# Strip 1's first product by sets, three of them at two levels, and four tiles of attention normalised on ScalarE

## The chip, the cores and the metric

The kernel runs on one core of a Trainium2 chip. A core has a matrix engine (TensorE, PE in the profile, with its weight loads as PEld), a vector engine (VectorE, DVE), an activation engine (ScalarE, ACT), GpSimd (POOL) and SyncE (SP), which here issues nearly all DMAs. Each engine works off its own instructions in order and waits on semaphores for the others. The metric is the device time of one launch in microseconds, lower is better.

## The reference

Everything is fp32. An attention block without softmax feeds a two-layer block with squared ReLU:

```python
kv  = einsum('bhsd,bhse->bhde', k, v)      # B=8, H=8, S=576, D=64
o   = einsum('bhsd,bhde->bhse', q, kv)
o   = o / sqrt(mean(o * o, axis=-1) + 1e-6) * g_norm
x   = o.transpose(0, 2, 1, 3).reshape(4608, 512)
g   = maximum(x @ w_in, 0) ** 2            # w_in  512 x 2048
out = g @ w_out                            # w_out 2048 x 512
```

## The kernel before

The 4608 tokens are cut into 36 tiles of 128, and four tiles make a strip of 512; there are nine strips, 0 to 8. The loop runs strip by strip: the first product of a strip (x by w_in, then relu and square), then its second product (by w_out). While a strip's products run, the attention for the next strip's tiles is worked in between them.

**Products with fewer multiplications.** Both products use a scheme that replaces eight block products by seven, at the price of sums of the inputs and of the results. The seven are numbered and done in the order 1, 2, 6, 5, 7, 3, 4; 1, 6 and 5 leave a partial sum that is copied out of PSUM to a `snap` buffer by ScalarE, and the later ones are added to it. The scheme can be used on two levels: each of the seven is then itself done by seven smaller ones. Strip 0's first product is plain. Strip 1's first product is done at one level by `up(s, g, p)`: four column groups g of w_in, in each the seven products p, each eight matmuls 128x128 by 128x256 in the trace (L839). ScalarE copies (L849), VectorE adds (L902) and squares (L903), ScalarE does relu and square for one quarter (L907, L908). From strip 2 on, the first product is done at two levels by `up_slot`: 55 slots, the outer products as seven sets in the order 1, 6, 7, 5, 2, 3, 4, in each set seven small products of eight matmuls 128x128 by 128x128 (`up_small`, L1283), one in every other slot, neighbouring sets overlapping. In those strips VectorE and GpSimd add (L1295), ScalarE copies (L1300) and does all relu and square (L1233, L1234). The second product is done at two levels from strip 1 on by `down_deep` (matmuls at L1066), which draws small products of its own into slots 49, 51 and 53 of the strip's first product.

**Sums of the weights.** For the two-level first product, GpSimd makes sums of w_in (`deep_sums_in`, seven calls in strip 1, tiles w_i, three instructions each), which SyncE stores to DRAM (`w_in_deep`, L1194 and L1196). Strips from 2 on load them again with `stream()`, the same function that loads the blocks of w_out and their sums; all of these tiles are called w_blk or w_i and share a pool of six buffers. Sums and differences of x (`leaf_x`, tiles x_l and x_t, `deep_differences_in` for w_in) are made by GpSimd and VectorE ahead of their use.

**Attention.** Its pieces stand in a list `slices`, and `attend(n)` works the list off up to number n. For batch 2, whose queries are tiles 9 to 12, and for tile 8, left over from batches 0 and 1, the pieces are: `query_means` for tile 8; `key_value` (K in the list) for the first and second pair of heads; four `transposed_query` (T), each a VectorE transpose of a q tile (L384); `roots_normalized`; `features` for tile 8 (four TensorE transposes, L636, and a ScalarE copy, L637, straight into the strip's x); `key_value` for the other heads; and then for tiles 9 and 10, and again for 11 and 12: `query` (64 matmuls 64x64 into x_ps, L468, then squares on ScalarE, L477), `mean_roots`, `normalized` (reciprocal roots and two VectorE multiplications, L563), `squares_x` (a VectorE transpose by 32x32 blocks, L643), and `send_x` (a store to DRAM, L652, which also puts `fetch_x`, four loads into the strip's x, on a list with a due time). From batch 3 on `normalized` is replaced by `inverse` and `scaled_heads`: eight ScalarE instructions of 128x64 per tile (L570).

**What sets the order.** The program's order on each engine is written by hand. In strip 1 each step of the first product moves a clock on, and after it the strip works off its share of the list:

```python
attend(begun + (goal - begun) * min(i + 1, 25) // 25)
```

Loads of k and v come from a list `keys_due`, one per step where due; loads of q from `drips`, spaced by the same clock. A q tile is loaded by four DMAs (L123) into one of three buffers; `load_q_rest` (L176) loads the left-over queries by eight small ones. All go through SyncE's one queue, in program order, in which also stand the stores of `deep_sums_in` and of `store_deep_sums` (L969, L975), the stores of results (L952) and the loads of weights. Eight semaphores are used in turn for its DMAs, so that an instruction also waits for the DMA eight before it.

Of the kernel before, what the change touches and what calls it, by code (L numbers as in the profile page):

```python
# [20 lines left out]
def kernel(  # L21
# [34 lines left out]
    nc = tc.nc  # L56
# [593 lines left out]
    def send_x(n):  # L650
        d = sent[n] = dram.tile([P, 4, NP, SQ], FP32, name="x_d", tag="x_d", bufs=2 * NT)
        nc.sync.dma_start(out=d, in_=squared.pop(n))  # L652
        tiles_due.append((clock[0] + {9: 30, 10: 36, 11: 24}.get(n, 6), fetch_x, (n,)))
# [53 lines left out]
    slices += [(T, (2, 2)), (T, (2, 3)), (features, (last[0],)), (K, (2, 2, 3))]  # L707
    pair_ends = []
    for b in range(2, B):
        pairs = query_pairs(b)  # L710
        for i, pair in enumerate(pairs):
            left = len(pairs) - i
            more = b + 1 < B
            at = left + (b == 2)
            keys = (b + 1, *{2: (0, 1), 1: (2, 3)}[at]) if more and at < 3 else ()
            if i == 0 and b > 2:
                slices += [(T, (b, p)) for p in (2, 3)]
            if i == 0 and b == 3:
                slices.append((K, (3, 2, 3)))
            if more and b > 2 and left == 1 + b % 2:  # L720
                slices.append((T, (b + 1, 0)))
            slices.append((query, (pair, *keys)))
            if b == 2:
                slices += [(T, (3, 1))] * (left == 1) + [(mean_roots, (pair,)), (normalized, (pair,))]
                slices += [(T, (3, 0))] * (left == 2) + [(squares_x, (n,)) for n in pair]
                for n in pair:
                    slices.append((send_x, (n,)))
                    if n % NT == NT - 1:
                        ready[n // NT] = len(slices)
                pair_ends.append(len(slices))  # L730
# [12 lines left out]
            if more and left == 1:  # L743
                slices.append((T, (b + 1, 1)))
# [144 lines left out]
    def up(s, g, p):  # L889
        open_bank(p)  # L890
        rhs = {
            1: halves(s, 0, 0), 2: halves(s, 1, 0), 3: halves(s, 1, 1),
            4: xc[s][3], 5: xc[s][0], 6: xc[s][1], 7: xc[s][2],
        }[p]
        for i in range(2):
            product(p, i, lambda kc: w_in[:, kc, g, A_IN[p], ts(i, P)], lambda kc: rhs[:, :, kc, :], KH)
        dest = quarters(s, g)

        def relu_squared(q):
            def f(b, a):  # L900
                o = dest[q]
                nc.vector.tensor_tensor(out=o, in0=b, in1=a, op=ALU.add)  # L902
                nc.vector.scalar_tensor_tensor(out=o, in0=o, scalar=0.0, in1=o, op0=ALU.max, op1=ALU.mult)  # L903
            return f

        def last(b):
            nc.scalar.activation(dest[21], b, AF.Relu)  # L907
            nc.scalar.activation(dest[21], dest[21], AF.Square)  # L908

        combine(p, relu_squared(11), relu_squared(12), last, relu_squared(22))  # L910
# [191 lines left out]
    def down_deep(s, k, i):  # L1102
        p = DEEP_ORDER[k]
        if k == i == 0:
            stream()
# [21 lines left out]
        if k == 0 and s >= DEEP_UP:  # L1127
# [52 lines left out]

    def deep_sums_in(b):
# [59 lines left out]
    def up_slot(s, slot):  # L1241

        for n, p in enumerate(UP_SETS):
            i, odd = divmod(slot - 7 * n, 2)
            if not odd and 0 <= i < 7:
# [6 lines left out]
        if s == DEEP_UP and at == 0 and n < 7:  # L1252
# [80 lines left out]
    for s in range(N_STRIP):  # L1333
# [11 lines left out]
        else:  # L1345
            steps = [(1, up, (s, g, p)) for g in range(NG) for p in ORDER]
# [12 lines left out]
        for i, (w, fn, a) in enumerate(steps):  # L1359
# [33 lines left out]
            if s:  # L1393
                clock[0] += 3.2 if i >= n_up else 2.2 if s == DEEP else 1.2
# [5 lines left out]
                elif not due(keys_due) and not (soon and due(tiles_due)):  # L1400
                    least = 2.1 if s == DEEP else 4.5 if i < n_up else 3.3
                    quiet = n_up * 2 // 3 < i < n_up + 3 or s == DEEP and i > n_up + 9
# [4 lines left out]
                if s == DEEP:  # L1407
                    attend(begun + (goal - begun) * min(i + 1, 25) // 25)
# [6 lines left out]
                if s == DEEP and i == n_up - 3:  # L1415
                    leaf_sums(s, 4)
                if s == 1 and i in range(2, 23, 3):
                    deep_sums_in((1, 6, 5, 4, 0, 2, 3)[i // 3])
                if s == 1 and i in (17, 20, 21, 23):
# [60 lines left out]
```

## Time and profile before

| what | value |
|---|---|
| time, median of three runs | 887.08 us (886.7 to 888.0) |
| the profiled execution: time, span | 886.17 us, 884.4 us |
| TensorE busy | 876.4 us (99%), 8296 matmuls |
| VectorE busy | 721.9 us (82%) |
| ScalarE busy | 351.8 us (40%) |
| GpSimd busy | 307.6 us (35%) |
| DMA | 235.73 MB, mean 267 GB/s |
| strip 1's first product | from 138.6 us |
| strip 2's first product, whole | from 236.8 us, its first slots drawn into strip 1's second product |

Busy times are shares of the span of one execution. The list of waits names, for an engine and a line, what ended its idle time there, with the total, the number and the longest. The chain of waits follows the work that ended last. A timeline gives, for one engine, start, duration and instruction, and in brackets the idle time before it with what ended it; for TensorE a run of matmuls is one row, whose duration reaches to the modelled end of its last, so that the distance between the starts of two rows is the rate.

### The profile page before, as it was taken

Reading aid. Unit: us, or ns where it says so; the run is one execution under the profiler, and the core shown is the slowest. Engines: PE = TensorE matmul, PEld = TensorE weight load, DVE = VectorE, ACT = ScalarE, POOL = GpSimd, SP = SyncE. Lnnn points to the kernel's source line nnn. Section 1 sums busy time; section 2 is a strip of 40 time slices with the busy share of each in tenths; the row PEclk is TensorE's granted clock in tenths of the full one; section 3 lists DMA queues with packets and bytes.
Section 4 is the critical chain, followed back from the end, with each engine's and each line's share of the span. In section 5 each row is a group of like instructions: output and inputs, shape, how many; then the busy total and the mean of one; then the engine's idle time right before and its main releaser. Section 6 shows DMA issues by size and latency. Waiting matters only on the chain.

```text
span 884.4 us, 20899 instructions
## 1 busy us (share of the span) xinstructions
PE 876.4 (99%) x8296; PEld 822.1 (93%) x8296; DVE 721.9 (82%) x1239; ACT 351.8 (40%) x805; POOL 307.6 (35%) x316
## 2 busy tenths in 40 slices
PE   8999999999999999999999999999999999999998
PEld 7445888889999999999999999999999999999998
DVE  4999998879778985798778966897888778866887
ACT  4898242320048203740365034902491147102710
POOL 0000005610549133631474045604570447044700
PEclk9999999999999999999999999999999999999999
DMA  9998997999969996989677978897668765884482
GB/s 306 321 314 252 299 376 222 289 346 353 301 186 278 327 330 214 227 323 314 208 216 293 314 237 244 286 319 244 207 218 303 255 212 184 294 292 164 178 314 105
DMA packets 170257, 235.73 MB, mean 267 GB/s; under 512 B 79536, under 2 KB 134576, under 8 KB 161840
## 3 DMA queue, kind: packets, MB, share of 16 engines
q1 hardware_dynamic: 169856, 234.33, 81.0%
q8 instruction: 65, 1.06, 0.5%
q14 instruction: 32, 0.26, 0.1%
q10 hardware_dynamic: 304, 0.07, 0.0%
HBM read 197.66 MB, written 36.70 MB: 265 GB/s over the span
## 4 chain that ended last, share of the span: by engine, by line
PE 95%; DVE 2%; ACT 2%; issue 0%; POOL 0%; DVEq 0%; POOLq 0%
PE ps_B L1066 22%; PE ps_A L1283 19%; PE ps_A L1066 17%; PE ps_B L1283 9%; PE ps_A L839 6%; PE ps_C L1283 5%; PE ps_B L839 3%; PE kv_ps L432 2%; PE ps_A L880 2%; PE x_ps L468 2%; PE ps_C L839 2%; PE ps_C L880 2%; PE ps_B L880 1%; PE ps_A L617 1%; ACT gt L1234 0%
## 5 line engine op out<-in xcount | busy, mean ns | idle before, releaser
L1066 PE MATMUL ps_B<-w_blk,g_s 128*128 128x128 f32 x1008 | 123.9, 275 | 0.0
L1066 PEld LDWEIGHTS ps_B<-w_blk,g_s 128*128 128x128 f32 x1008 | 118.1, 192 | 0.1
L1283 PE MATMUL ps_A<-x_l,w_in 128*128 128x128 f32 x784 | 103.8, 275 | 0.3 <-ACT snap L1300 0.3
L289 POOL TENSOR_TENSOR x_l<-xT 128x256 f32<-128x256 f32 x21 | 15.7, 747 | 236.7 <-PE ps_A L1066 187.8
L1283 PEld LDWEIGHTS ps_A<-x_l,w_in 128*128 128x128 f32 x784 | 95.4, 192 | 0.6 <-ACT snap L1300 0.5
L1066 PE MATMUL ps_B<-w_blk,gt 128*128 128x128 f32 x752 | 95.2, 275 | 0.0
L1066 PE MATMUL ps_A<-w_blk,g_s 128*128 128x128 f32 x768 | 93.6, 275 | 0.0
L1066 PEld LDWEIGHTS ps_B<-w_blk,gt 128*128 128x128 f32 x752 | 89.6, 192 | 0.1
L1066 PEld LDWEIGHTS ps_A<-w_blk,g_s 128*128 128x128 f32 x768 | 89.6, 192 | 0.0
L1295 POOL TENSOR_TENSOR snap<-snap,gt 128x512 f32<-128x512 f32 x35 | 45.8, 1309 | 118.8 <-ACT snap L1300 103.7
L1300 ACT COPY snap<-ps_A 128x512 f32<-128x512 f32 x63 | 36.9, 585 | 109.7 <-PE ps_A L1283 98.0
L1233 ACT ACTIVATE gt<-gt 128x512 f32<-128x512 f32 x112 | 70.1, 625 | 12.8 <-DVE gt L1295 12.7
L1066 PE MATMUL ps_A<-w_blk,gt 128*128 128x128 f32 x576 | 72.2, 275 | 0.0
L1234 ACT ACTIVATE gt<-gt 128x512 f32<-128x512 f32 x112 | 70.7, 631 | 3.6
L1066 PEld LDWEIGHTS ps_A<-w_blk,gt 128*128 128x128 f32 x576 | 68.2, 192 | 0.0
L1082 ACT COPY o_sb<-ps_A 128x128 f32<-128x128 f32 x24 | 6.4, 265 | 148.4 <-PE ps_A L1066 148.4
L1081 DVE TENSOR_TENSOR o_sb<-o_sb,ps_B 128x256 f32<-128x256 f32 (+1 forms) x123 | 47.5, 386 | 16.9 <-ACT o_sb L1082 12.0
L289 DVE TENSOR_TENSOR gt<-gt 128x2048 f32<-128x2048 f32 (+1 forms) x29 | 59.7, 2064 | 0.0
L1295 POOL TENSOR_TENSOR gt<-gt,snap 128x512 f32<-128x512 f32 x42 | 52.3, 1273 | 17.8 <-DVE snap L1295 17.8
L1283 PE MATMUL ps_B<-x_l,w_blk 128*128 128x128 f32 x392 | 52.1, 276 | 0.0
L1283 PE MATMUL ps_A<-x_l,w_blk 128*128 128x128 f32 x392 | 51.9, 275 | 0.0
L1081 DVE TENSOR_TENSOR o_sb<-o_sb,ps_A 128x256 f32<-128x256 f32 (+1 forms) x96 | 37.2, 387 | 15.1 <-ACT o_sb L1082 10.5
(193 smaller groups left out, 1822.3 us busy)
## 6 DMA issues: line engine op xcount, KB each, us to landing
w_blk<-w_deep SPq DMA_DIRECT2D x56, 1024.0 KB, 6.6
w_blk<-w_out SPq DMA_DIRECT2D x56, 768.0 KB, 6.0
w_blk<-w_in_deep SPq DMA_DIRECT2D x49, 768.0 KB, 5.3
raw<-in_moe_w_in_dram SPq DMA_DIRECT2D x16, 512.0 KB, 7.1
raw<-in_moe_w_out_dram SPq DMA_DIRECT2D x16, 512.0 KB, 6.1
k<-in_k_dram SPq DMA_DIRECT2D x29, 256.0 KB, 4.6
v<-in_v_dram SPq DMA_DIRECT2D x29, 256.0 KB, 5.0
x_d<-x_q SPq DMA_DIRECT2D x27, 256.0 KB, 4.6
```

The source lines that it names most:

```text
L289: eng.tensor_tensor(out=out, in0=a, in1=b, op=ALU.subtract)
L432: nc.tensor.matmul(ps[ts(h, D), i], lhsT=a, rhs=w, start=i == 0 and c == 0, stop=c == C, skip_group_check=True)
L468: nc.tensor.matmul(ps[half, r, i, ts(p, D)], lhsT=q[row, half], rhs=kvd[b, p][row, row], start=True, stop=True)
L839: nc.tensor.matmul(bank[BANK[p]][:, i, :], lhsT=lhsT(k), rhs=rhs(k), start=p in (1, 5, 2) and i == 0 and k == 0, stop=k == n - 1, skip_gro ...
L880: nc.tensor.matmul(ps, lhsT=w_in[:, kc % KH, g, kc // KH * 2 + fh, ts(i, P)], rhs=xt[0][:, :, kc, :], start=kc == 0, stop=kc == NP - 1,)
L1066: nc.tensor.matmul(chain[c][x][:, i, :], lhsT=a[:, f, :], rhs=w[:, f, :], start=x not in opened[c] and f == 0, stop=f == FQ // 2 - 1, skip ...
L1081: add = lambda out, a, b: nc.vector.tensor_tensor(out=out, in0=a, in1=b, op=ALU.add)
L1233: nc.scalar.activation(o, o, AF.Relu)
L1234: nc.scalar.activation(o, o, AF.Square)
L1283: nc.tensor.matmul(ps[:, i, :], lhsT=w, rhs=rhs, start=j in (1, 2, 5) and i == 0, stop=True, skip_group_check=True)
L1295: add = lambda eng, out, a, b: eng.tensor_tensor(out=out, in0=a, in1=b, op=ALU.add)
L1300: nc.scalar.copy(t, ps)
```

## The change

1. **Strip 1's first product.** `up` is replaced by `up_set`: 16 steps, the sets 1, 6, 7 and 5 one after the other over the four column groups, each one product of eight matmuls (in the trace's counting) into a bank of its own, followed by one ScalarE copy (set 1), one VectorE addition (6 and 7) or two additions with relu and square on ScalarE (5). Sets 2, 3 and 4 are done as in later strips by `up_slot`, slots 28 to 54, 21 small products; the first of them are drawn in among the last `up_set` steps, and the small products of the second product come into slots 49, 51 and 53 of strip 1 too.
2. **Sums.** The w_i tiles for sets 2, 3 and 4 are kept in the pool of six as strip 1's own weights besides being stored. The seven `deep_sums_in` come at other steps and in another order; some `leaf_x` and `deep_differences_in` move into strip 1. A 2048-wide VectorE addition in strip 1's second product goes; GpSimd makes it in parts.
3. **Tile 8** goes by `squares_x`, `send_x` and `fetch_x` in place of `features`.
4. **Tiles 9 to 12** are normalised by `inverse` and `scaled_heads`, as later tiles are, in place of `normalized`.
5. **Loads and pace.** In strip 1 up to two entries of `keys_due` are loaded per step, and the list of attention pieces is spaced over 23 parts of the first product in place of 25 steps, an `up_set` counting as one part and a small product as half.

The core of the diff:

```diff
-        tiles_due.append((clock[0] + {9: 30, 10: 36, 11: 24}.get(n, 6), fetch_x, (n,)))
+        tiles_due.append((clock[0] + {8: 50, 9: 30, 10: 36, 11: 24}.get(n, 6), fetch_x, (n,)))
...
-    slices += [(T, (2, 2)), (T, (2, 3)), (features, (last[0],)), (K, (2, 2, 3))]
+    slices += [(T, (2, 2)), (squares_x, last), (T, (2, 3)), (send_x, last), (K, (2, 2, 3))]
...
-                slices += [(T, (3, 1))] * (left == 1) + [(mean_roots, (pair,)), (normalized, (pair,))]
-                slices += [(T, (3, 0))] * (left == 2) + [(squares_x, (n,)) for n in pair]
+                slices += [(T, (3, 1))] * (left == 1) + [(mean_roots, (pair,)), (inverse, (pair,))]
+                slices += [(scaled_heads, (pair, t, r)) for t in range(2) for r in range(2)]
+                slices += [(T, (3, 0))] * (left == 2)
                 for n in pair:
-                    slices.append((send_x, (n,)))
+                    slices += [(squares_x, (n,)), (send_x, (n,))]
...
-    def up(s, g, p):
...
+    def up_set(s, g, p):
+        rhs = {1: lambda: halves(s, 0, 0), 5: lambda: xc[s][0], 6: lambda: xc[s][1], 7: lambda: xc[s][2]}[p]()
+        ps = fpsum.tile([P, 2, TH], FP32, name="ps_D", tag="f")
+        for i in range(2):
+            for kc in range(KH):
+                nc.tensor.matmul(
+                    ps[:, i, :], lhsT=w_in[:, kc, g, A_IN[p], ts(i, P)], rhs=rhs[:, :, kc, :],
+                    start=i == kc == 0, stop=kc == KH - 1, skip_group_check=True,
+                )
         dest = quarters(s, g)
+        add = lambda q, a: nc.vector.tensor_tensor(out=dest[q], in0=ps, in1=dest[a], op=ALU.add)
+        if p == 1:
+            nc.scalar.copy(dest[11], ps)
+        elif p == 5:
+            add(22, 21)
+            add(12, 12)
+            nc.scalar.activation(dest[22], dest[22], AF.Relu)
+            nc.scalar.activation(dest[22], dest[22], AF.Square)
+        else:
+            add(*{6: (12, 11), 7: (21, 12)}[p])
...
-            if k == 0:
-                nc.vector.tensor_tensor(out=q12, in0=q12, in1=q22, op=ALU.add)
...
+            if UP_SETS[4:].count(IN_SET[b]):
+                w_blk["in", DEEP, IN_SET[b]] = whole.rearrange("p n f e -> p n (f e)")
...
-            steps = [(1, up, (s, g, p)) for g in range(NG) for p in ORDER]
+            x_sums[s, 4] = xc[s][3]
+            by_set = [(2, up_set, (s, g, p)) for p in UP_SETS[:4] for g in range(NG)]
+            small_ones = [(1, up_slot, (s, slot)) for slot in range(28, 55)]
+            steps = by_set[:13] + small_ones[:1] + by_set[13:14] + small_ones[1:3] + by_set[14:15]
+            steps += small_ones[3:5] + by_set[15:] + small_ones[5:]
+            small_steps = {28, 30, 32, 34, *range(35, 55)}
+            work = [2 if fn == up_set else a[1] in small_steps for _, fn, a in steps]
+            passed = [sum(work[: i + 1]) / 2 for i in range(len(steps))]
...
-                clock[0] += 3.2 if i >= n_up else 2.2 if s == DEEP else 1.2
+                clock[0] += 3.2 if i >= n_up else 1.1 * work[i] if s == DEEP else 1.2
...
-                elif not due(keys_due) and not (soon and due(tiles_due)):
+                elif not (due(keys_due) and (s > DEEP or due(keys_due) or True)) and not (soon and due(tiles_due)):
...
-                    attend(begun + (goal - begun) * min(i + 1, 25) // 25)
+                    attend(begun + (goal - begun) * min(int(passed[min(i, n_up - 1)]), 23) // 23)
...
-                if s == 1 and i in range(2, 23, 3):
-                    deep_sums_in((1, 6, 5, 4, 0, 2, 3)[i // 3])
+                if s == DEEP and i in (1, 3, 5, 7, 10, 12, 15):
+                    deep_sums_in({1: 6, 3: 2, 5: 3, 7: 1, 10: 5, 12: 4, 15: 0}[i])
```

More of the change, by code (lines that the diff above doesn't have):

```diff
@@ L887, in up_first @@
             nc.scalar.activation(dest[(11, 12, 21, 22)[2 * fh + th]][:, i, :], ps[:, ts(th, TH)], AF.Square)
-    def up(s, g, p):
[L890 to L894, printed above, removed]
-        for i in range(2):
-            product(p, i, lambda kc: w_in[:, kc, g, A_IN[p], ts(i, P)], lambda kc: rhs[:, :, kc, :], KH)
-        dest = quarters(s, g)
[L899 to L910, printed above, removed]
+    def up_set(s, g, p):
+        rhs = {1: lambda: halves(s, 0, 0), 5: lambda: xc[s][0], 6: lambda: xc[s][1], 7: lambda: xc[s][2]}[p]()
+        ps = fpsum.tile([P, 2, TH], FP32, name="ps_D", tag="f")
+        for i in range(2):
+            for kc in range(KH):
[3 more added lines that the diff above has]
+                )
+        dest = quarters(s, g)
+        add = lambda q, a: nc.vector.tensor_tensor(out=dest[q], in0=ps, in1=dest[a], op=ALU.add)
[8 more added lines that the diff above has]
+            add(*{6: (12, 11), 7: (21, 12)}[p])
     for p, t in zip((1, 2, 5), w_first):
@@ L1103, in down_deep @@
         p = DEEP_ORDER[k]
-        if k == i == 0:
+        if k == i == 0 and s >= DEEP_UP:
             stream()
@@ L1126, in down_deep @@
             return
-        if k == 0 and s >= DEEP_UP:
+        if k == 0:
             if i == 0:
@@ L1179 @@
     w_half = lambda b, kc, f: w_in[:, kc, 2 * f : 2 * f + 2, b]
+    IN_SET = {b: p for p, b in A_IN.items()}
     def deep_sums_in(b):
@@ L1244, in up_slot @@
             i, odd = divmod(slot - 7 * n, 2)
-            if not odd and 0 <= i < 7:
+            if not odd and 0 <= i < 7 and (s > DEEP or n >= 4):
                 up_small(s, n, p, ORDER[i], slot)
@@ L1251, in up_slot @@
             leaf_x(s, n + 1)
-        if s == DEEP_UP and at == 0 and n < 7:
+        if at == 0 and n < 7 and (s == DEEP_UP and n < 4 or s == DEEP and n > 4):
             deep_differences_in(A_IN[UP_SETS[n]])
@@ L1399 @@
                         f(*a)
-                elif not due(keys_due) and not (soon and due(tiles_due)):
+                elif not (due(keys_due) and (s > DEEP or due(keys_due) or True)) and not (soon and due(tiles_due)):
                     least = 2.1 if s == DEEP else 4.5 if i < n_up else 3.3
-                    quiet = n_up * 2 // 3 < i < n_up + 3 or s == DEEP and i > n_up + 9
+                    quiet = s > DEEP and n_up * 2 // 3 < i < n_up + 3
+                    quiet = quiet or s == DEEP and (i > n_up + 9 or i < n_up + 3 and passed[min(i, n_up - 1)] > 19)
                     quiet = quiet or s == DEEP and i < n_up and drips and drips[0][0] == load_q_rest
@@ L1414 @@
                     next(last_sums, None)
-                if s == DEEP and i == n_up - 3:
-                    leaf_sums(s, 4)
-                if s == 1 and i in range(2, 23, 3):
-                    deep_sums_in((1, 6, 5, 4, 0, 2, 3)[i // 3])
-                if s == 1 and i in (17, 20, 21, 23):
+                if s == DEEP and i in (1, 3, 5, 7, 10, 12, 15):
+                    deep_sums_in({1: 6, 3: 2, 5: 3, 7: 1, 10: 5, 12: 4, 15: 0}[i])
+                if s == DEEP and i == 8:
+                    leaf_x(s, 4)
+                if s == DEEP and i == 9:
+                    deep_differences_in(2)
+                if s == DEEP and i in (18, 22):
                     stream()
```

## The prediction

> **What bounds the kernel now.** I read the page first.
>
> ```profile
> span 884.4 us, 20899 instructions
> ...
> PE 876.4 (99%) x8296; PEld 822.1 (93%) x8296; DVE 721.9 (82%) x1239; ACT 351.8 (40%) x805; POOL 307.6 (35%) x316
> ...
> PEclk9999999999999999999999999999999999999999
> ...
> PE 95%; DVE 2%; ACT 2%; issue 0%; POOL 0%; DVEq 0%; POOLq 0%
> ```
>
> TensorE is busy for 99% of the span, at the full granted clock in all 40 slices, and carries 95% of the chain that ended last. So every microsecond of matmul that goes is a microsecond, and so is every new wait of TensorE: there is no idle time in which one could hide. The list of TensorE's waits shows how little it waits now (columns: total us, times, longest).
>
> ```profile
> PE t_ps L376 <- POOL ident masks.py:199: 1.4, 1, 1.4
> ...
> PE ps_A L1283 <- ACT snap L1300: 0.3, 1, 0.3
> ```
>
> Then I read the stretch that changes, strip 1's first product, in TensorE's timeline (start, duration, instruction) beside the small products of strip 2.
>
> ```profile
> 151.47 1.89 PE L839 MATMUL ps_A<-x_t,w_in 128*128 128x256 f32 x8
> 153.20 1.89 PE L839 MATMUL ps_A<-xT,w_in 128*128 128x256 f32 x8
> ...
> 156.65 0.60 PE L636 MATMUL xt_ps<-ident,x_n 128*128 128x128 f32 x4
> 157.09 1.89 PE L839 MATMUL ps_A<-x_t,w_in 128*128 128x256 f32 x8
> ...
> 265.55 1.06 PE L1283 MATMUL ps_A<-x_l,w_in 128*128 128x128 f32 x8
> 266.44 1.06 PE L1283 MATMUL ps_B<-x_l,w_blk 128*128 128x128 f32 x8
> ```
>
> From start to start, a one-level product costs 1.73 us, a small one 0.89 us, tile 8's four transposes 0.44 us. Next I asked what batch 2's first query (tiles 9 and 10) rests on: the chain of waits and VectorE's timeline.
>
> ```profile
> 162.37 0.86 PE x_ps L468 x48
> 163.22 0.04 issue
> 163.26 0.46 PE x_ps L468 x16
> ```
>
> ```profile
> 162.49 0.71 DVE L384 STREAM_TRANSPOSE qT<-q 128x512 f32<-128x512 f32 x1 [3.21 <-DMA q<-in_q_dram]
> ```
>
> The last 16 matmuls of x_ps read batch 2's fourth transposed query. VectorE sat 3.21 us for its DMA, finished at 163.20, and TensorE started at 163.26. Query and load meet to the tenth of a microsecond: the cover has no slack. SyncE's timeline shows who issues that load, among what.
>
> ```profile
> 153.43 1.04 SPq L123 DMA_DIRECT2D q<-in_q_dram  x2
> 154.56 0.60 SPq L1196 DMA_DIRECT2D w_in_deep<-w_i  x1
> 155.22 6.41 SPq L123 DMA_DIRECT2D q<-in_q_dram  x6
> ```
>
> **The change, part by part.** *Matmuls.* Of strip 1's 28 one-level products 16 stay, regrouped by set; 12 go, and 21 small ones come: 21 x 0.893 - 12 x 1.73 = 18.75 - 20.76 = -2.0 us. Tile 8's transposes go: -0.44. Together **-2.4 us**, on the path. It fails only if something else stops TensorE.
>
> *The pace of the attention work.* Strip 1 works off its list of slices in 25 equal parts, one for each step; now in 23 parts, and the list has grown, because one `normalized` has become an `inverse` and four `scaled_heads`. By my count of the list the query of tiles 9 and 10 is slice 10 of 24 before and slice 11 of 32 after: it came after 11 products (24 x 11 / 25 reaches 10), and comes after 8 (32 x 8 / 23 reaches 11). TensorE therefore reaches those 16 matmuls 3 x 1.73 + 0.44 = 5.6 us earlier, at about 157.6. What they wait for does not move: up to that load SyncE's queue holds the same instructions in the same order (four q, eight q_rest, an output, four q, a stored sum of w_in, two pairs of k and v, two q, another stored sum, two q). Three kinds of them wait for another engine: the stored sums for GpSimd, k and v for a key/value product that frees their buffers, the first q for a transpose; all three now come in earlier steps, and SyncE reaches its instructions no sooner, because each DMA in front still takes its time: SyncE's longest wait between 128 and 185 us is 1.3 us, for a q tile behind this one. The DMA engines are 0.92 to 1.12 busy in each 3 us from 150 to 162. The key/value product just ahead of the query (its k and v are issued from 150.7 to 153.3, median landing 4.6 and 5.0 us) will show part of the same wait. **+5.6 us**. Bounds: with the median landing of a q load (4.2 us) after its issue near 156.5 it would be ready near 161.4 with the transpose, 1.8 earlier, 3.8 left; with tile 8's transpose (0.70, new on VectorE in front of it) in its way, 6.3. I take 5.6, the load's own row. Behind VectorE's waiting transpose stand the additions that empty the set products' banks; TensorE waits at the same time, so they cost nothing more.
>
> *ScalarE.* The rows:
>
> ```profile
> L570 ACT ACTIVATE x_n<-x_ps,newton 128x64 f32<-128x64 f32 x184 | 40.8, 338 | 7.3 <-DVE newton L500 7.2
> ...
> L1233 ACT ACTIVATE gt<-gt 128x512 f32<-128x512 f32 x112 | 70.1, 625 | 12.8 <-DVE gt L1295 12.7
> ...
> L1300 ACT COPY snap<-ps_A 128x512 f32<-128x512 f32 x63 | 36.9, 585 | 109.7 <-PE ps_A L1283 98.0 <-DVE root L496 3.9 <-DMA out_dram<-o_sb 2.9
> ```
>
> Back to back a head costs 40.8 / 184 = 0.22 us. Four tiles get 8 heads each, 7.1 us, and VectorE loses four of L563 at 0.69. In strip 1 all relu and square of the small sets come too (VectorE's L903 did half of it before, 12.2 us that go). Between slots 34 and 50, 15 products long or 13.4 us, ScalarE has 16 heads 3.5, nine pairs of relu and square 11.3, two squares 1.1, two copies 1.2: 17.1 us, 3.7 more than TensorE gives it. The last product of set 4's first half (slot 50) reuses a bank that such a copy must have read, and the copy stands behind the heads. Before, that form of wait cost 0.3 us. Tile 12's heads have a wait of their own, for the store of tile 10's transposed x (a pool of three buffers), which SyncE issues behind GpSimd's sums. The slack of the slots in between takes most of the 3.7; I take a third, **+1.2 us**, bounds 0 and 3.0.
>
> *What other work hides.* VectorE is 19.0 of 25 us busy from 140 to 165 and gets less. GpSimd gets three sums of x (nine instructions near 0.75 us) and an addition of 1.3, 8 us in all, and had 29.6 of 50 us taken from 140 to 190 (its timeline). Sums for sets 2, 3 and 4 stay in their buffers, and strip 1 needs no loads for them. Tile 8 takes five more DMAs through SyncE (4.6 us to land for the store), due long before strip 2 at 236.8. Should GpSimd fall behind, its stored sums hold SyncE and w_blk behind them: a rival below.
>
> *Clock.* The granted clock is 1.00 throughout, but the longest wait of TensorE in this trace is 1.4 us, so no row shows a wait like the new one; I count nothing. [...]
>
> **Sum.** -2.4 + 5.6 + 1.2 = +4.4 us. The profiled execution took 886.17 us (span 884.4 and 1.8 around it), so 890.6; it lies 0.9 below the median of 887.08, so by the median **891.5 us**. The likeliest case's own range is -2.4 + 3.8 + 0 = +1.4 to -2.4 + 6.3 + 3.0 = +6.9: 888.5 to 894.0. The bound for no change is 0.2%, 1.8 us.
>
> **Rivals.** *The matmuls win* (faster, 0.13): the q load comes earlier. It would have to be transposed by 157.6 to cost nothing, by 160.0 to break even without a ScalarE wait. For it: VectorE sits idle ahead of it, and its issues lie 6 us before it lands, above the 4.2 median. Against: the queue's order and the full DMA engines. Time: 884.7 without waits, 885.9 with ScalarE's. *A draw* (0.10): half of the q wait, and no other: 887.08 - 2.4 + 2.8 = 887.5. *A second late load* (slower still, 0.15): the three second products drawn into slots 49 to 53 need a w_blk whose load waits until slot 38 has freed a buffer, 11 slots or 9.8 us ahead, against 6.0 to 6.6 us to land, and in the queue it stands behind GpSimd's last sums (three stored parts, each made in about 1.4 us by L1189 and L289), as does the store that tile 12's heads wait for. If GpSimd or the queue is late by more than the 3.2 us left, each further us is one of TensorE's: I price it at 3, 894.5. A smaller form of "doesn't do what it says", small products slower than 0.89 in strip 1, takes back at most the 2.0 us: 893.5, inside the range.
>
> **The numbers.** The likeliest, q wait with some of ScalarE's: 0.62. Faster comes from the first rival, 0.13; same from the second, 0.10; slower 0.77. The range runs from 885.5, which takes in the upper half of the first rival, to 895.5, which takes in most of the third; about 0.17 is left out.
>
> **What would show it.** Right: in the changed profile TensorE's waits name x_ps for the transposed q with 3 to 5 us, kv_ps for k or v with 1 to 2, the two together near 5.6, and a small product for a ScalarE copy near 1.2 about 57 us after strip 1's first product; TensorE's busy time 2.4 us lower. Wrong: x_ps waits under 2 us, or a load of w_blk, a sum of GpSimd or a clock below 1 ends a longer wait.

## The result and the profile after

The changed kernel is slower: 890.41 us against 887.49 us, medians of 19 runs each, ratio 1.0035 with a 95% interval of 1.0023 to 1.0047, so about 3 us. Ratios are taken over fast runs; one run behind this document was a slow one, of the experiment e8_rest_later below, at 1728 us, and the median there is 885.26 us without it. The profiled execution took 890.47 us (span 888.7), 4.3 us more than the profiled execution of the kernel before, which lies 1.3 us below the median of its 19 runs; that is why traces differ by more than medians do.

The page of the changed kernel, at the places that were shown of the kernel before:

```profile
span 888.7 us, 21121 instructions
...
PE 876.2 (99%) x8364; PEld 823.5 (93%) x8364; DVE 719.0 (81%) x1245; ACT 369.1 (42%) x855; POOL 320.8 (36%) x332
...
PEclk9999999899999999999999999999999999999999
...
PE 79%; DVE 8%; ACT 5%; DMA 5%; issue 2%; SPq 1%; POOL 1%; DVEq 0%; ACTq 0%; POOLq 0%
```

TensorE's share of the chain falls from 95% to 79%. That share does not measure the loss: 16% of the span are 142 us, and the execution is 4.3 us longer. Followed back from the end, the chain leaves TensorE at the waits of strip 1 and runs on through earlier work of the other engines. In one of the 40 slices the granted clock is below 9 tenths. The list of TensorE's waits has new heads:

```profile
PE kv_ps L432 <- DMA v<-in_v_dram: 2.2, 2, 1.1
PE x_ps L468 <- DVE qT L384: 1.8, 1, 1.8
PE t_ps L376 <- POOL ident masks.py:199: 1.4, 1, 1.4
PE ps_A L1284 <- ACT snap L1301: 1.1, 2, 0.8
```

TensorE's timeline through the place:

```profile
148.29 7.07 PE L895 MATMUL ps_D<-x_t,w_in 128*128 128x256 f32 x32
156.44 0.69 PE L432 MATMUL kv_ps<-v,k 128*64 128x64 f32 x16 [1.08 <-DMA v<-in_v_dram]
158.27 0.69 PE L432 MATMUL kv_ps<-v,k 128*64 128x64 f32 x16 [1.15 <-DMA v<-in_v_dram]
...
162.55 0.71 PE L468 MATMUL x_ps<-kv_all,qT 64*64 64x64 f32 x16 [1.75 <-DVE qT L384]
163.19 10.22 PE L895 MATMUL ps_D<-x_t,w_in 128*128 128x256 f32 x40
173.24 1.05 PE L1284 MATMUL ps_A<-xT,w_in 128*128 128x128 f32 x8
...
199.09 1.13 PE L1284 MATMUL ps_A<-x_l,w_in 128*128 128x128 f32 x8 [0.82 <-ACT snap L1301]
```

The key/value product and the query of tiles 9 and 10 now come after eight products, at 155.4 us, and stop three times: once for each of the two pairs of k and v, and once for the fourth transposed q. VectorE's timeline has the same wait from the other side, now 6.41 us long. VectorE comes to it 3.9 us earlier than before (at 155.37 in place of 159.28), and the load lands only 0.7 us earlier:

```profile
161.78 0.71 DVE L384 STREAM_TRANSPOSE qT<-q 128x512 f32<-128x512 f32 x1 [6.41 <-DMA q<-in_q_dram]
```

SyncE, which issues these loads, is where it was. Its first k of the pair, in the kernel before and in the changed one:

```profile
150.72 0.38 SPq L132 DMA_DIRECT2D k<-in_k_dram  x1
```

```profile
150.95 0.38 SPq L132 DMA_DIRECT2D k<-in_k_dram  x1
```

The five products behind the query start at 163.19 and are done at 173.24: 10.05 us in place of 5 x 1.73 = 8.65. The table by stretches (its column after the five engines is the granted clock) shows what goes with it:

```profile
core 0: us, PE busy (x) PEld busy (x) DVE busy (x) ACT busy (x) POOL busy (x), PEclk, DMA share, GB/s
155.40:163.20 7.80, 3.86 (x105) 3.41 (x105) 1.42 (x3) 0.52 (x2) 6.46 (x7) 0.73 1.14 328
163.20:168.00 4.80, 4.80 (x20) 4.03 (x17) 2.53 (x5) 1.08 (x2) 0.00 (x0) 0.72 1.08 276
168.00:173.20 5.20, 5.20 (x26) 4.58 (x25) 3.76 (x10) 2.76 (x13) 2.38 (x2) 1.00 1.10 307
```

TensorE is busy for half of the first stretch, and in that and in the next the granted clock is 0.73 and 0.72. In steps of 2 us it is 0.52, 0.50 and 0.50 from 159 to 165, then 0.78 and 1.00.

**The account of strip 1.** From its first product to strip 2's first matmul of its own (L1283 before, L1284 after, xT by w_in) the kernel before takes 236.79 - 138.63 = 98.16 us, the changed one 242.04 - 138.90 = 103.14: +4.98. The key/value product and the query end at 163.19; without a wait and at the full clock they would end at 148.29 + 4 x 1.73 + 0.15 for the change of shape (the row of the four lasts 7.07 us, not 6.92) + 1.46 + 1.35 (the kernel before, 158.91 to 160.37 and 162.30 to 163.65) = 158.2, so this place costs 5.0 us, of which 4.0 is idle and 1.0 matmuls on a slow clock. Most of that 1.0 lies ahead of the wait for the fourth q, and TensorE would have waited there longer had it been quicker. Only the last 16 matmuls, behind the q, count against the clock: 163.19 - 162.55 = 0.64 us, in place of 163.65 - 163.26 = 0.39 in the kernel before. So the late loads cost 4.75 us and the clock 0.25 here. The five products behind cost 1.4 by the clock, which makes 1.65 for the clock in all, and ScalarE's copy 0.8. With -2.0 for the matmuls (below) the sum is +5.2, against the +4.98 measured. At strip 2's first matmul the changed kernel is 242.04 - 236.79 = 5.25 behind, at the end 4.3; of the 0.9 that comes back, 0.4 is a wait of the kernel before for VectorE (at 289 us) that no longer shows, and the rest was not traced.

### The profile page after: what moved, and what is told of

Its sections match the earlier page's. It is cut to its first block, busy times and chain, and to the rows that moved or that the text cites. A ratio compares the mean times of both kernels' runs of the same rounds, so it can differ in the third digit from the quotient of the medians.

```text
span 888.7 us, 21121 instructions
## 1 busy us (share of the span) xinstructions
PE 876.2 (99%) x8364; PEld 823.5 (93%) x8364; DVE 719.0 (81%) x1245; ACT 369.1 (42%) x855; POOL 320.8 (36%) x332
## 3 DMA queue, kind: packets, MB, share of 16 engines
q8 instruction: 66, 1.08, 0.5%
## 4 chain that ended last, share of the span: by engine, by line
PE 79%; DVE 8%; ACT 5%; DMA 5%; issue 2%; SPq 1%; POOL 1%; DVEq 0%; ACTq 0%; POOLq 0%
PE ps_B L1065 22%; PE ps_A L1284 19%; PE ps_A L1065 17%; PE ps_B L1284 10%; PE ps_C L1284 5%; PE ps_D L895 2%; DVE w_t L289 2%; PE x_ps L468 2%; PE kv_ps L432 2%; DMA q<-in_q_dram 1%; DMA w_deep<-w_t 1%; DVE w_in L289 1%; DMA raw<-in_moe_w_in_dram 1%; ACT raw L254 1%; DVE wt L289 1%
## 5 line engine op out<-in xcount | busy, mean ns | idle before, releaser
L1284 PE MATMUL ps_A<-x_l,w_in 128*128 128x128 f32 x832 | 110.3, 275 | 1.1 <-ACT snap L1301 1.1
L1284 PEld LDWEIGHTS ps_A<-x_l,w_in 128*128 128x128 f32 x832 | 101.2, 192 | 1.6 <-issue 1.0
L1296 POOL TENSOR_TENSOR snap<-snap,gt 128x512 f32<-128x512 f32 x38 | 50.4, 1327 | 126.6 <-ACT snap L1301 119.3
L1234 ACT ACTIVATE gt<-gt 128x512 f32<-128x512 f32 x124 | 77.6, 626 | 12.3 <-DVE gt L1296 12.1
L1235 ACT ACTIVATE gt<-gt 128x512 f32<-128x512 f32 x124 | 78.2, 631 | 3.9
L1174 POOL TENSOR_TENSOR gt<-gt 128x512 f32<-128x512 f32 x32 | 52.8, 1671 | 0.0
L1284 PE MATMUL ps_A<-x_l,w_blk 128*128 128x128 f32 x392 | 52.1, 276 | 0.0
L1284 PE MATMUL ps_B<-x_l,w_blk 128*128 128x128 f32 x392 | 52.0, 276 | 0.0
```

The source lines that it names most:

```text
L1174: nc.gpsimd.tensor_tensor(out=a, in0=a, in1=b, op=ALU.add)
L1234: nc.scalar.activation(o, o, AF.Relu)
L1235: nc.scalar.activation(o, o, AF.Square)
L1284: nc.tensor.matmul(ps[:, i, :], lhsT=w, rhs=rhs, start=j in (1, 2, 5) and i == 0, stop=True, skip_group_check=True)
L1296: add = lambda eng, out, a, b: eng.tensor_tensor(out=out, in0=a, in1=b, op=ALU.add)
```

## The experiments

The two theories were these. *Theory*: the loss sits in one place of strip 1, where TensorE meets k, v and q before they have landed, and in the clock behind it. *Rival*: it is spread, over 50 more ScalarE instructions, 16 more of GpSimd and the tile that goes through DRAM.

**The changed kernel again.**

> The changed kernel, unaltered, as the other side of that comparison. Theory: ratio 1.003 to 1.005, and in its profile the waits for k, v and q with a granted clock below 1 behind them. Rival: a ratio of 1.000 here would make the whole loss a matter of the chip.

Measured: 891.33 us, ratio 1.0035 (1.0022 to 1.0048). The same loss again, and the same waits in the profile: kv_ps 2.5, x_ps 1.9, ScalarE's copy 1.1. The granted clock was 0.83 from 160 to 170 us and 1.00 in the windows of 10 us on either side: by that, an estimate, it cost at most 10 x 0.17 = 1.7 us.

**The early query alone, in the kernel before.**

```diff
-                    attend(begun + (goal - begun) * min(i + 1, 25) // 25)
+                    attend(begun + (goal - begun) * min(i + 1, 18) // 18)
```

> The kernel before, with its list of pieces spaced over 18 steps of strip 1 instead of 25, so that the key/value product comes after 7 and the query of tiles 9 and 10 after 8 of the one-level products, as early as in the changed kernel. All arithmetic is that of the kernel before. Theory: this alone brings the waits for k, v and the transposed q, 4 to 5.5 us of them, and a clock below 1 behind them, 0 to 1.5 us: ratio 1.004 to 1.008. Rival (spread loss): the early query costs nothing by itself, 1.000.

Measured: 894.33 us, ratio 1.0072 (1.0057 to 1.0087). TensorE's waits:

```profile
PE kv_ps L432 <- DMA v<-in_v_dram: 3.0, 1, 3.0
PE ps_A L839 <- DVE gt L902: 3.0, 2, 2.8
```

The early pace costs by itself more than the whole change, with the kernel before's own products. But it is not a clean copy of the case: here q came in time (transposed at 159.17), with one of GpSimd's sums stored ahead of it in place of two; k and v did not. The pieces that followed too fast filled VectorE's queue, one of them a transpose that waited 1.31 us for the next late q tile (at 170.03), so that an addition behind them held TensorE for 2.8 us. Pace has two ends, loads ahead of it and VectorE behind it. The rival's 1.000 is out: an early query does cost. That nothing else in the changed kernel costs is not shown by this run; e8_rest_later below bears on it.

**The late query in the changed kernel.**

```diff
-                    attend(begun + (goal - begun) * min(int(passed[min(i, n_up - 1)]), 23) // 23)
+                    at, n_sl = min(int(passed[min(i, n_up - 1)]), 23), goal - begun
+                    attend(begun + (min(n_sl * at // 23, 9) if at < 11 else 10 + (n_sl - 10) * (at - 10) // 13))
```

> The changed kernel with the key/value product and the query of tiles 9 and 10 held back until 11 products of strip 1 have passed, as many as before the change (8 in the changed kernel); the list of pieces catches up over the steps that are left. All matmuls are the same. Theory (TensorE meets k, v and the fourth transposed q too early, waits 4.0 us for them, and the granted clock falls to a half for some microseconds after it, about 1.4 us more): both vanish, no wait of x_ps for qT over 0.5 us, clock 1.00 in every window; what is left is -2.4 of matmuls and about +1 of ScalarE: 1.5 us below the kernel before, 885 to 886.5, ratio near 0.998. Rival (the loss is spread: the 50 more ScalarE instructions, 16 more of GpSimd and the tile that goes through DRAM slow the other engines all along): the time stays near the changed kernel's, ratio 1.0035, whatever becomes of the wait.

Measured: 892.22 us, ratio 1.0055 (1.0043 to 1.0067): slower still, and the expected gain is nowhere. The waits at the first query did go; they came up again one key/value product later:

```profile
179.31 0.69 PE L432 MATMUL kv_ps<-v,k 128*64 128x64 f32 x16 [2.80 <-DMA v<-in_v_dram]
181.10 0.69 PE L432 MATMUL kv_ps<-v,k 128*64 128x64 f32 x16 [1.11 <-DMA v<-in_v_dram]
...
200.27 1.13 PE L1284 MATMUL ps_A<-x_l,w_in 128*128 128x128 f32 x8 [1.76 <-ACT snap L1301]
```

The next loads of k and v take the buffers that the first key/value product frees, and the program puts them into SyncE's queue only behind that product. In the changed kernel the product ends near 159 and they are issued from 165.0. Here it ends near 162 and they are issued from 173.4, with six loads of q and five stores ahead of them that stood behind them before, while the next product comes at 176.5. SyncE hardly waited for the buffers themselves (its rows show no idle time ahead of these four loads, and in the changed kernel none of 0.2 us or more ahead of a load of k or v from 128 to 195 us): it is their place in the order that made them late. The clock fell there too (0.83 from 180 to 190 us), and the pieces pressed into the remaining steps made ScalarE's copy 1.76 us late. My theory had the place of the loss right and the remedy wrong: holding the consumer back moves the loads that take its buffers back as well, and further.

**The loads forward, first way: two stores behind the q tile.**

```diff
-        nc.sync.dma_start(
+        store = lambda: nc.sync.dma_start(
             out=w_in_deep[b].rearrange("p n g e -> p n (g e)"), in_=whole[:, 0:3].rearrange("p n f e -> p n (f e)")
         )
+        if b in (6, 2):
+            held.append(store)
+        else:
+            store()
...
+                while s == DEEP and i == 5 and held:
+                    held.pop(0)()
```

> The changed kernel with the stores of the first two sums of w_in (768 KB each) issued after the loads of the fourth q tile instead of before; the pace and all other work are the same. Theory: the q tile lands later than TensorE wants it because SyncE's queue holds 1.5 MB of stores ahead of it; at the 300 GB/s of this stretch they take 5 us, so the transposed q comes 3 to 5 us earlier, k and v about 2.5 us earlier, the waits of kv_ps and x_ps fall from 4.0 us together to under 1, the clock stays at 1.00: ratio near 0.998. If it is not the queue but the small packets of the q loads themselves, the q tile still comes near 162 us and the wait of x_ps stays over 1.5 us: ratio 1.002 or more. The rival of a spread loss expects 1.0035.

Measured: 886.19 us, ratio 0.999 (0.9972 to 1.0007). VectorE's timeline, and the first of TensorE's waits:

```profile
158.71 0.71 DVE L384 STREAM_TRANSPOSE qT<-q 128x512 f32<-128x512 f32 x1 [3.49 <-DMA q<-in_q_dram]
```

```profile
PE kv_ps L432 <- DMA v<-in_v_dram: 1.5, 1, 1.5
```

The q tile is 3.1 us earlier, x_ps does not wait, and the clock is 1.00 in all windows from 140 to 290 us. Of the changed kernel's waits 1.5 us for a v and ScalarE's 1.1 are left: the first k was issued only 0.8 us sooner (150.18), where I had expected k and v 2.5 us earlier. Here what stood ahead of the q tile in SyncE's queue set its landing, by 3.1 us.

**The loads forward, second way: the left-over queries behind them.**

```diff
-            if i == n_up + 12:
-                load_q_rest(2, nc.sync)
...
             done += w
+            if s == DEEP and i == 7:
+                load_q_rest(2, nc.sync)
```

> The changed kernel with the eight small loads of batch 2's left-over queries issued after the fourth q tile and its neighbours (step 7 of strip 1) instead of ahead of all of them; they held SyncE for 5 us while the DMA engines were under a fifth busy. Nothing else is moved. Theory (what sets the wait is the place of the k, v and q loads in SyncE's queue): k, v and q land up to 5 us earlier, no wait of kv_ps or x_ps over 0.5 us before 170 us, clock 1.00; -2.4 of matmuls and about +1 of ScalarE are left, ratio 0.998. Rival: k and v are held by the buffers that the key/value product before frees, and q by the DMA engines; then the waits shrink by less than half and the ratio stays over 1.0015.

Measured: 885.52 us, ratio 0.9969 (0.9953 to 0.9984): faster than the kernel before. TensorE's waits, with what is left of the new ones:

```profile
PE ps_A L1284 <- ACT snap L1301: 1.1, 2, 0.8
...
PE x_ps L468 <- DVE qT L384: 0.4, 1, 0.4
```

What held the queue can be read in SyncE's timeline of the changed kernel:

```profile
142.60 5.02 SPq L176 DMA_DIRECT2D q_rest<-in_q_dram  x8
```

Eight loads of 16 KB each keep SyncE for 5.0 us, while the kernel before moved 10 to 38 GB/s for some 4 us of that stretch (its DMA row, in slices of 0.75 us); in the changed one the DMA engines were 0.21 to 0.24 busy in each us from 144 to 148. Without them ahead, SyncE issues the k at 147.19 in place of 150.95:

```profile
147.19 0.38 SPq L132 DMA_DIRECT2D k<-in_k_dram  x1
```

Strip 1, from first product to strip 2, is now 236.63 - 139.32 = 97.31 us, 0.85 less than before the change; take its 0.37 and 0.82 us of waits out, and the matmuls are worth -2.0 us. The 50 ScalarE and 16 GpSimd instructions and the tile through DRAM are all still there, so a loss spread over them is out.

**The same, beside the changed kernel.**

> The kernel of e8_rest_later again, on the same chip and beside the same runs as the changed kernel and e11_tile12_later. Theory: ratio 0.997 to 0.998 as before, and 0.5 to 0.7 per cent below the changed kernel: waits of 4.0 us for k, v and q and 1.4 us of lost clock in 890 are 0.6 per cent. Rival (the difference between e8_rest_later and the changed kernel came from the chips they ran on): within 0.2 per cent of the changed kernel.

Measured: 886.48 us, ratio 0.9979 (0.9967 to 0.9990); against the 891.33 us of the changed kernel on the same chip 0.5% less. So the order of eight small loads is worth 4.8 us in the changed kernel.

**And in the kernel before.**

> The kernel before with the eight small loads of left-over queries at the same later place as in e8_rest_later. Theory: in the kernel before, the fourth q tile arrives just when TensorE wants it, so that earlier loads gain nothing, and the ratio is 1.000. If the ratio falls below 0.999, the order of these loads is a gain of its own, and the gain of e8_rest_later is not the change's.

Measured: 886.81 us, ratio 0.9989 (0.9976 to 1.0003). No gain that can be told from none. The interval reaches down to 2.1 us, so a small one is not excluded; the 4.8 us are there only where the query has moved forward.

**The clock by itself.** 26 matmuls whose results are never read, each counted as two in the trace (x20 and x32), fill the waits.

```diff
+            if ns[0] == 9 and p == NP - 1:
+                keep_busy(ps[:, 0, 0, ts(p, D)], 16)
...
+        if (b, ps_of[0]) == (2, 2):
+            keep_busy(ps[:, 0], 10)
```

> The changed kernel with 26 matmuls of the identity by 64 columns that compute nothing used: 10 ahead of the key/value product of batch 2's last heads, 16 ahead of the query's last 16 matmuls, where TensorE waits for its loads anyway. The output is the same. Theory: the granted clock fell to a half behind the wait because TensorE did little for some 6 us; with the wait filled it stays at or near 1.00 from 155 to 175 us, the loads land as before, and the time falls by the 1 to 1.5 us that five products took too long: ratio 1.002. Rival (the clock is not what costs; the loads alone set the end): the time stays, 1.0035, or rises by the dummies' own 2 us, 1.006.

Measured: 890.47 us, ratio 1.0023 (1.0009 to 1.0036). Its timeline and its windows:

```profile
159.68 3.79 PE L376 MATMUL x_ps<-ident 128*128 128x64 f32 x32
163.39 0.46 PE L472 MATMUL x_ps<-kv_all,qT 64*64 64x64 f32 x16
163.79 8.90 PE L899 MATMUL ps_D<-x_t,w_in 128*128 128x256 f32 x40
172.52 1.05 PE L1288 MATMUL ps_A<-xT,w_in 128*128 128x128 f32 x8
```

```profile
150.00:160.00 10.00, 10.00 (x135) 9.08 (x133) 5.02 (x7) 0.52 (x2) 9.61 (x9) 1.00 1.11 315
160.00:170.00 10.00, 10.00 (x77) 9.14 (x76) 6.53 (x15) 1.95 (x7) 1.75 (x3) 1.00 0.83 243
```

The clock stays at 1.00 and the five products take 172.52 - 163.79 = 8.73 us, 1.3 less than in the changed kernel. The mean clock is 1.000 in all 12 runs, whose times lie within 2.3 us of one another; the 19 of the changed kernel lie within 5.8. The dummies were too many: the q tile was transposed at 161.85, and they ran on to 163.39. So the part of the clock is shown in the profile; in the medians the intervals of the two kernels overlap, and a gain of 0.1% is likely but not certain. The q tile itself came about as before the dummies, transposed at 161.85 against 162.49.

**ScalarE's part, first try: all four tiles on VectorE.**

```diff
-                slices += [(scaled_heads, (pair, t, r)) for t in range(2) for r in range(2)]
+                slices += [(scaled, (pair, 0)), (no_piece, ()), (scaled, (pair, 1)), (no_piece, ())]
```

> The changed kernel with tiles 9 to 12 multiplied by their norms on VectorE again (two instructions of 128x512 per pair, in place of 32 of ScalarE in all), at the same pace of the list. Theory: the wait of a small product for a ScalarE copy in strip 1 (1.1 us in the profile) goes, the waits for k, v and q stay: 0.5 to 1.1 us less than the changed kernel, ratio 1.0025. Rival (it was VectorE that held strip 1 up, and the move to ScalarE pays for itself): slower than the changed kernel, ratio over 1.004.

Measured: 891.08 us, ratio 1.0039 (1.0027 to 1.0051): no gain. The 0.8 us wait for ScalarE became one for VectorE:

```profile
PE ps_B L1285 <- DVE snap L1297: 0.8, 1, 0.8
...
PE ps_A L1285 <- ACT snap L1302: 0.3, 1, 0.3
```

**Second try, on top of the better load order: tile 12 alone on VectorE.**

```diff
+                if left == 2:
+                    slices += [(scaled_heads, (pair, t, r)) for t in range(2) for r in range(2)]
+                else:
+                    slices += [(scaled_heads, (pair, 0, r)) for r in range(2)] + [(scaled, (pair, 1)), (no_piece, ())]
```

> The same as e8_rest_later, and tile 12 alone multiplied by its norms on VectorE (one instruction) in place of eight ScalarE instructions, at the same pace. Theory: ScalarE is about 1 us behind when the copy of set 4's partial sum is due, and eight instructions fewer are 1.8 us; that wait goes and no VectorE wait comes: 0.8 us less than e8_rest_later, ratio 0.997. Rival (VectorE is as full there): a wait for a VectorE sum of 0.8 us takes its place, as in e4_dve_scaled, and the ratio is that of e8_rest_later.

Measured: 888.86 us, ratio 1.0005 (0.9993 to 1.0016), 0.4% worse than without it. VectorE's timeline, and TensorE's:

```profile
189.19 0.69 DVE L563 TENSOR_TENSOR x_n<-x_ps,newton 128x512 f32<-128x512 f32 x1 [3.26 <-ACT x_n L570]
```

```profile
190.54 1.16 PE L1288 MATMUL ps_B<-xT,w_i 128*128 128x128 f32 x8 [2.04 <-DVE snap L1300]
```

VectorE's piece stood in its queue for 3.26 us behind ScalarE's heads, which were late, and the addition behind it emptied a bank too late. TensorE lost 2.0 us, and the clock was 0.50 from 193 to 195. This execution also waits 1.1 us for a v and 1.2 for w_blk, which were not followed.

**Third try: tile 12's heads in strip 2.**

```diff
+                slices += heads[: 2 * left]
...
+                    slices += heads[2:] * (left == 1 and n == pair[1])
```

> The same as e8_rest_later, and the eight ScalarE heads, the transpose and the store of tile 12 put behind the pieces that strip 2 needs (tile 12 belongs to strip 3), so that they run in strip 2's first product; the pace of the other pieces is the same. Theory: ScalarE's backlog of about 1 us at slot 50 is those heads (1.8 us); the wait of 0.8 us for its copy goes and nothing takes its place: 0.8 us below e8_rest_later, ratio 0.996. Rival (the copy waits for other work, relu and square of sets 2 and 3, which fill ScalarE by themselves): the wait stays, or one as long comes in strip 2, where ScalarE takes the heads instead; ratio 0.997.

Measured: 890.45 us, ratio 1.0030 (1.0017 to 1.0042). The ScalarE wait shrank to 0.3, and the same 2.04 us for a VectorE sum came, behind another piece that had slid forward in the list, tile 11's transpose:

```profile
189.70 0.71 DVE L643 STREAM_TRANSPOSE x_q<-x_n 128x512 f32<-128x512 f32 x1 [3.25 <-ACT x_n L570]
```

A wait of 1.4 us for w_blk and one of 1.1 for a VectorE result (o_sb) stand beside it and were not followed.

**Fourth try: the same with that piece kept in its place.** Two empty pieces stand where the heads stood.

> As e11_tile12_later (on top of e8_rest_later, tile 12's eight ScalarE heads moved behind strip 2's pieces), but with two empty pieces where the heads stood, so that tile 11's VectorE transpose keeps its place among VectorE's additions. Theory: in e9_rest_split and e11_tile12_later a VectorE piece slid forward in the list, sat 3.25 us in VectorE's queue for ScalarE's heads, and the addition behind it held TensorE for 2.0 us; here that wait does not come, the 0.8 us wait for ScalarE's copy in strip 1 goes too, and the ratio is 0.996 to 0.997. Rival (what cost there was work itself, put on the wrong engine or strip): the 2.0 us wait stays, or one like it comes in strip 2, ratio 0.999 or more.

Measured: 888.60 us, ratio 1.0005 (0.9989 to 1.0021). Half of the theory held. The transpose no longer waits and the 2.04 us are gone; but TensorE's list has

```profile
PE ps_B L1068 <- DMA w_blk<-w_deep: 2.2, 2, 1.6
PE ps_B L1287 <- DVE snap L1299: 1.5, 1, 1.5
```

VectorE was not idle for a moment ahead of that sum. Its timeline, then e8_rest_later's for the same additions, then GpSimd's of the first and, for the same addition, of e8_rest_later:

```profile
192.79 1.37 DVE L289 TENSOR_TENSOR g_s<-gt,g_s 128x512 f32<-128x512 f32 x1
194.09 0.68 DVE L1299 TENSOR_TENSOR gt<-ps_A,gt 128x512 f32<-128x512 f32 x1
194.69 1.16 DVE L289 TENSOR_TENSOR g_s<-gt 128x512 f32<-128x512 f32 x1
```

```profile
192.41 0.67 DVE L289 TENSOR_TENSOR g_s<-gt,g_s 128x512 f32<-128x512 f32 x1
193.00 0.68 DVE L1296 TENSOR_TENSOR gt<-ps_A,gt 128x512 f32<-128x512 f32 x1
193.60 0.67 DVE L289 TENSOR_TENSOR g_s<-gt 128x512 f32<-128x512 f32 x1
```

```profile
192.34 1.28 POOL L1299 TENSOR_TENSOR snap<-snap,gt 128x512 f32<-128x512 f32 x1 [1.83 <-ACT snap L1304]
193.57 5.09 POOL L1177 TENSOR_TENSOR gt<-gt 128x512 f32<-128x512 f32 x3
```

```profile
193.61 1.80 POOL L1296 TENSOR_TENSOR snap<-snap,gt 128x512 f32<-128x512 f32 x1 [3.48 <-ACT snap L1301]
```

With the copies of ScalarE earlier, GpSimd starts earlier, and VectorE's additions of two SBUF operands take 1.2 to 1.4 us beside it instead of 0.67; the one with a PSUM operand stays at 0.68. The late loads of w_blk (292 and 385 us) cannot be put down to this edit: e8b_rest_later, without it, waits 1.1 us for one at 383 us. ScalarE's 0.8 us is thus not a loss that lies open: of four ways of taking it away none gained, and the three on top of the better load order cost time. The best version found is the changed kernel with the left-over queries loaded later.

## Why the prediction was right, point by point

- **Matmuls, -2.4 us.** Measured -2.0, from e8_rest_later less its waits. Right in kind; where the other 0.4 us go was not traced, changes of shape, which the sum did not count, being one candidate (in the kernel before, a product behind matmuls of another shape took 1.83 us in place of 1.73, 163.65 to 165.48). TensorE's busy time, forecast 2.4 us lower, fell by 0.2 only, because the matmuls were busy longer on the slow clock, by the 1.0 and the 1.4 us of the account above.
- **The query comes after 8 products and its load does not move, +5.6 us.** Right, and it is the cause: 4.75 us in the profile, inside the bounds of 3.8 to 6.3. It is less than 5.6 because the q tile was transposed at 162.5, 0.7 us ahead of the kernel before. The split among the waits was off: k and v 2.2 and q 1.8, where I had written 1 to 2 and 3 to 5, because the two pairs of k and v came each too late. An x_ps wait under 2 us was one of my signs of being wrong, and together the waits were 4.0 us, not near 5.6; the rest of the delay is matmuls on a slow clock between the waits.
- **The clock, counted at nothing.** This term was mis-sized. It cost 1.4 us in the five products behind the wait and 0.25 in the end of the query, 1.65 together, and at most 1.7 by the estimate for e12_changed_again. The trace of before, with no wait over 1.4 us and a granted clock of 1.00, had no row that gave it a price. Here the clock fell at 159 us, behind waits of 1.08 and 1.15, and the longest one, of 1.75, came when it was already at 0.50; with the waits filled, in e7_busy, it stayed at 1.00.
- **ScalarE, +1.2 us.** 0.8 at the very place, slot 50's copy behind the heads; ScalarE ran from 188.7 to 199 without a gap of note. Right, slightly oversized.
- **What other work hides.** Right: no wait for GpSimd or for w_blk in strip 1 of the changed kernel. The third rival did not come there. Waits for w_blk came in seven of the other runs, 0.2 to 2.2 us in all, the longer ones at 290 us or later; the changed kernel itself has 0.4 at 387 us in e12_changed_again.
- **The sum, +4.4 us.** The traces differ by 4.3, the medians by 2.9. So close a hit is partly luck: the loads cost 0.85 less than forecast, ScalarE 0.4 less, the clock 1.65 more and the matmuls gained 0.4 less, which makes 5.2 in strip 1, and 0.9 came back later. That the terms add up in one execution and not in the medians has a visible part: over the 19 runs of the changed kernel the recorded mean clock goes from 1.000 (six runs, median 889.0 us) to 0.994 (three runs, median 893.4). The profiled run had 0.996. The waits and the fall of the clock are there in both profiled executions; the recorded clock says that how long it stays down differs from run to run. Six runs at 1.000 are only 1.5 us above the median of the kernel before, less than the terms without the clock give (2.6), and no trace of such a run was taken.
- **The rivals.** "The matmuls win" named its own condition, a q tile ready by 157.6 to 160.0. e2_stores_behind_q and e8_rest_later bring it to 159.4 and 158.6, and end near or below the kernel before, as that rival said.

## What to carry to other kernels

When attention pieces, or any side work, are spaced by their share of a list, adding pieces to the list moves all the others; compute for each consumer the time at which it now comes, and set it beside the landing time of its loads, which sit in a queue that did not move (here VectorE came to the q tile 3.9 us earlier and the tile landed 0.7 us earlier). If a load is late, move the load, here by taking eight small ones out of its way, before holding the consumer back: where the next loads take the consumer's buffers, they move back with it (in e1_later_query from 165.0 to 173.4 us). A piece that waits for another engine holds up what stands behind it on its own (in e9_rest_split VectorE's wait of 3.26 us became one of 2.04 for TensorE), so its place in the list is part of its cost.

## What the runs showed of the hardware

- In the changed kernel TensorE was busy for 1.77 of the 4 us from 155 to 159 and waited 1.08 and 1.15 us there; the granted clock was 1.00 until 159 us, then 0.52, 0.50, 0.50 and 0.78 in the four windows of 2 us up to 167, with a wait of 1.75 us from 160.8. Behind one wait of 2.04 us it fell for a shorter time in e9_rest_split (0.80, 0.50 and 0.85 in the three 2 us windows from 191) and not at all in e11_tile12_later (1.00 throughout), at the same place. In e3_before_early it was 1.00 from 150 to 170 us, with a wait of 3.02 us there, and 0.66 from 170 to 180, with one of 2.81 us, behind which eight matmuls took 3.78 us in place of 1.89. In these runs the length of a single wait alone did not decide.
- An fp32 VectorE addition of 128x512 with both operands in SBUF takes 0.67 us alone (e8_rest_later, 192.41) and, when a GpSimd addition is already running, 1.16 to 1.80 (e13_tile12_apart, 194.69 and 189.26). In the whole trace of the changed kernel such instructions take 0.62 to 0.69 us alone and 0.69 to 1.79, 1.16 in the median, beside one that is running; with one operand in PSUM they take at most 0.69 either way. Where the two began together (e8_rest_later, 193.60 and 193.61), VectorE's took 0.67 and GpSimd's 1.80 in place of 1.28.
- Eight loads of 16 KB occupied SyncE for 5.0 us, 0.43 each in the median and 1.66 for the longest; two stores of 768 KB took it 0.43 and 0.46. With those stores out of the way the q tile came 3.1 us earlier, more than the 0.9 us that SyncE was spared; the other 2.2 us, by my estimate, are their transfer.
